# Packing masked score triangles of sliding-window attention as 64-key halves on 32x64 array tiles

## The chip, the cores and the metric

The kernel runs on one core of one Trainium2 chip. The metric is the device time of one launch in microseconds. Times quoted are medians of several runs. A ratio is the mean time of one kernel's runs over that of the other's of the same rounds, so it is not quite the ratio of the medians quoted beside it. Intervals are 95% intervals.

## The reference

A transformer layer on 2048 tokens of width 1024: layer norm, attention with 32 heads of 32 columns in which a query sees itself and the 255 keys before it, output projection, residual; then layer norm, a feed-forward block of width 3584 with silu, residual. Everything is bf16.

```python
scores = jnp.einsum("bhqd,bhkd->bhqk", q, k) * (Dh ** -0.5)
idx = jnp.arange(S)
mask = (idx[:, None] - idx[None, :] >= 0) & (idx[:, None] - idx[None, :] < W)   # W = 256
p = _softmax(jnp.where(mask[None, None], scores, -1e9), axis=-1)
o = jnp.einsum("bhqk,bhkd->bhqd", p, v)
# ...
h = x + _A_ref(_layernorm(x, axis=-1), A_wqkv, A_wo)
h2 = h + _B_ref(_layernorm(h, axis=-1), B_w1, B_w2)
```

## The kernel before

The tokens are four blocks of 512, numbered 0 to 3. The attention of block b is spread over the dense matmuls of another stage: those that make Q, K and V of block b + 1, and, for block 3, the output projection of blocks 0 to 2. Each such stage has 24 dense groups of 8 matmuls with 512 columns. Between the groups stand **score bursts** (keys times queries for four heads at once, on four 32-row tiles of the array), the exp on ScalarE, the masking selects on GpSimd, and the **output matmuls** (128x33, probabilities times values).

For 128 queries there are three chunks of 128 keys. The middle one is not masked; the first and the last are, each on one side of its diagonal. A group of four heads has 12 chunks of scores, which fill three bursts of 512 columns, called A, B and C:

```python
PIECES = {
    "A": [(0, 0, 3, 0), (-2, 0, 1, 3)],       # key tile, first query tile, tiles, column
    "B": [(-1, 0, 2, 0), (2, 2, 2, 2)],
    "C": [(3, 3, 1, 0), (1, 1, 3, 1)],
}
def scores(b, g, kind):
    for kt, q0, nq, ch in PIECES[kind]:
        t = b * 4 + kt
        for hh in range(4):
            r0 = hh * DH
            nc.tensor.matmul(sc[hh // 2][:, hh % 2, ch * P:(ch + nq) * P],
                             lhsT=kT[t // 4][r0:r0 + DH, g, (t % 4) * P:(t % 4 + 1) * P],
                             rhs=qT[b][r0:r0 + DH, g, q0 * P:(q0 + nq) * P],
                             start=True, stop=True, tile_position=(r0, 0))
    for pair in range(2):                      # two heads of 512 columns each
        nc.scalar.activation(out=e, in_=sc[pair], func=ACT.Exp, scale=scale)
        # ... selects for the masked chunks
```

The stage of block 3: its dense groups are the output projection. Each pair of groups makes one 128-row tile of h, which VectorE adds to the residual and the DMA queue of SyncE (SP) stores to DRAM. Four tiles of h are read back as one transfer of 1 MB for the layer norm of the first feed-forward block.

```python
def wo_group(b, j, c):                         # residual tile b*4+j, column half c
    # ... 8 dense matmuls into one of two accumulators
    nc.vector.tensor_tensor(out=t_out[j % 2][...], in0=acc, in1=r_in[(b * 4 + j) % 6][...], op=ALU.add)
    if c == 1:
        late.append(lambda: nc.sync.dma_start(out=h_dram[...], in_=t_out[j % 2]))
# ... stage of block 3, n counts its 24 groups
run_late()                                     # queued stores and transposes, first of all
if n % 2 == 0 and n >= 2 and n // 2 + 5 < S // P: load_res(n // 2 + 5) # a residual tile
scores(NB - 1, g, kind)
wo_group(*dense[n])
if pending: pending.pop(0)()                   # a piece of output matmuls
if n in (1, 4, 7, 12, 15): load_w1(...)        # 896 KB of weights each
if n == 9: steps = ln2_steps(0); steps.pop(0)()   # the 1 MB read of h
for _ in range(1 if n < 16 else 2):            # layer norm steps of the first feed-forward block
    if steps and n >= 12: steps.pop(0)()
```

The softmax here doesn't subtract the row's maximum and nothing guards it: scores larger than these inputs give would overflow.

Of the kernel before, what the change touches and what calls it, by code (L numbers as in the profile page):

```python
# [14 lines left out]
P = 128  # L15
# [3 lines left out]



PIECES = {
    "A": [(0, 0, 3, 0), (-2, 0, 1, 3)],
    "B": [(-1, 0, 2, 0), (2, 2, 2, 2)],
    "C": [(3, 3, 1, 0), (1, 1, 3, 1)],
}
CHUNKS = [
    [(-2, "A", 3), (-1, "B", 0), (0, "A", 0)],
    [(-1, "B", 1), (0, "A", 1), (1, "C", 1)],
    [(0, "A", 2), (1, "C", 2), (2, "B", 2)],  # L30
    [(1, "C", 3), (2, "B", 3), (3, "C", 0)],
]
KINDS = "ABC"


def first_stream(n_groups):
# [12 lines left out]
def kernel(  # L49
# [37 lines left out]
    r_t = big.tile([P, 4096], BF16, name="r_t")  # L87
    r_o = big.tile([P, 8192], BF16, name="r_o")
    r_a = big.tile([P, 49664], BF16, name="r_a")
    r_e = big.tile([P, 12288], BF16, name="r_e")  # L90
    r_n = big.tile([P, 1536], BF16, name="r_n")

    ps_tp = tc.tile_pool(name="ps_tp", bufs=1, space=bass.MemoryType.PSUM, reuse_waits="tile")
# [5 lines left out]
    def view(region, off, *dims):  # L99
        n = 1  # L100
        for d in dims:
            n *= d
        ap = region[:, off:off + n]
        if len(dims) == 2:
            return ap.rearrange("p (a b) -> p a b", b=dims[1])
        if len(dims) == 3:
            return ap.rearrange("p (a b c) -> p a b c", b=dims[1], c=dims[2])
        return ap
# [15 lines left out]
    w2_off = 18432  # L124
    w2 = [view(r_a, w2_off + 4096 * s, 4, D) for s in W2_SLOT]
    ebuf = [view(r_e, 1024 * i, 2, 512) for i in range(12)]
    obuf = [view(r_n, 512 * i, 4, P) for i in range(3)]
    h_blk = [view(r_a, w2_off + 4096 * 4, 4, D)] + [view(r_e, 8192, 4, D)] * 3
    ln2T = [view(r_a, w2_off + 4096 * 5, KT, 512), view(r_e, 0, KT, 512), view(r_e, 4096, KT, 512), view(r_e, 0, KT, 512)]
# [103 lines left out]
    def v_group(b, j, c, copy, between=None):  # L233
        acc = next_acc()
        for kt in range(KT):
            if between:
                between(kt)
            nc.tensor.matmul(acc, lhsT=lnT_b[b % 2][:, kt, j * P:(j + 1) * P], rhs=wv[:, kt, c * 512:(c + 1) * 512],  # L238
                             start=(kt == 0), stop=(kt == KT - 1))
        copy(out=v[:, b * 4 + j, c * 16:(c + 1) * 16, 0:DH], in_=acc.rearrange("p (h d) -> p h d", d=DH))  # L240

    def qk_group(b, which, g, copy, between=None):
        acc = next_acc()
        col0 = which * D + g * P
        for kt in range(KT):
            if between:
                between(kt)
            nc.tensor.matmul(acc, lhsT=wqk[:, kt, col0:col0 + P], rhs=lnT_b[b % 2][:, kt, :],  # L248
                             start=(kt == 0), stop=(kt == KT - 1))
        copy(out=(qT, kT)[which][b][:, g, :], in_=acc)  # L250
# [10 lines left out]
        while late:  # L261
            late.pop(0)()

    def wo_group(b, j, c):
        acc = next_acc()
        for g in range(G):
            nc.tensor.matmul(acc, lhsT=qT[b][:, g, j * P:(j + 1) * P], rhs=wo[:, g, c * 512:(c + 1) * 512],  # L267
                             start=(g == 0), stop=(g == G - 1))
        nc.vector.tensor_tensor(out=t_out[j % 2][:, c * 512:(c + 1) * 512], in0=acc,
                                in1=r_in[(b * 4 + j) % 6][:, c * 512:(c + 1) * 512], op=ALU.add)  # L270
        if c == 1:
            late.append(lambda: nc.sync.dma_start(out=h_dram[(b * 4 + j) * P:(b * 4 + j + 1) * P, :], in_=t_out[j % 2]))


    def e_of(i, kind, pair):
        return ebuf[(i * 6 + KINDS.index(kind) * 2 + pair) % 12]

    first_bursts, first_where = first_stream(G)

    def scores(b, g, kind):  # L280
        for kt, q0, nq, ch in PIECES[kind]:
            t = b * 4 + kt
            for hh in range(4):
                r0 = hh * DH
                nc.tensor.matmul(  # L285
                    sc[hh // 2][:, hh % 2, ch * P:(ch + nq) * P],
                    lhsT=kT[t // 4][r0:r0 + DH, g, (t % 4) * P:(t % 4 + 1) * P],
                    rhs=qT[b][r0:r0 + DH, g, q0 * P:(q0 + nq) * P],
                    start=True, stop=True, tile_position=(r0, 0),
                )  # L290
        for pair in range(2):
            e = e_of(b * G + g, kind, pair)
            nc.scalar.activation(out=e, in_=sc[pair], func=ACT.Exp, scale=scale)  # L293
            if kind == "A":
                mask(e, 0, 1, True)
                mask(e, 2, 2, False)
            elif kind == "B":
                mask(e, 1, 1, False)
                mask(e, 2, 1, True)
            else:  # L300
                mask(e, 0, 2, True)
                mask(e, 3, 1, False)

    def scores_first(n):
        ch = 0
# [19 lines left out]
                    mask(e, ch, 1, kt == q)  # L325

    def mask(e, c0, n, upper):
        ap = e[:, :, c0 * P:(c0 + n) * P].rearrange("p h (c q) -> p h c q", q=P)
        sgn = 1 if upper else -1
        nc.gpsimd.affine_select(out=ap, in_=ap, pattern=[[0, 2], [0, n], [sgn, P]],  # L330
                                compare_op=ALU.is_ge if upper else ALU.is_gt,
                                fill=0.0, base=0, channel_multiplier=-sgn)

    def attn_out(b, g, first, last):
        i = b * G + g
        for n in range(first, last):
            pair, qt, hh = n // 8, n // 2 % 4, n % 2
            for m, (kt, kind, ch) in enumerate(CHUNKS[qt]):
                nc.tensor.matmul(  # L339
                    o_ps[pair][:, qt * 2 + hh, 0:VW],  # L340
                    lhsT=e_of(i, kind, pair)[:, hh, ch * P:(ch + 1) * P],
                    rhs=v[:, b * 4 + kt, g * 4 + pair * 2 + hh, :],
                    start=(m == 0), stop=(m == 2),
                )
            if n % 8 == 7:
                attn_norm(i, pair)
# [26 lines left out]
    def attn_transpose(b, g):  # L373
        i = b * G + g
        nc.sync.dma_start_transpose(out=qT[b][:, g, :].rearrange("p (t q) -> p t q", q=P),
                                    in_=obuf[i % 3].rearrange("p t d -> p (t d)"))

    def tail_of(b, g):
        def end():
            attn_out(b, g, 11, 16)  # L380
            late.append(lambda: attn_transpose(b, g))
        return [lambda: attn_out(b, g, 0, 5), lambda: attn_out(b, g, 5, 11), end]

    dve, act = nc.vector.tensor_copy, nc.scalar.copy

# [71 lines left out]
    for j in range(4):  # L457
        load_x(2, j)
    steps, turns = ln1_steps(2)
    pending = []  # L460
    count = [0, 0]

    def between(kt):
# [21 lines left out]


    for b in range(2, NB):
        dense = [lambda j=j, c=c: v_group(b, j, c, dve) for j in range(4) for c in range(2)]
        dense += [lambda w=w, g=g: qk_group(b, w, g, dve) for g in range(G) for w in range(2)]
        if b + 1 < NB:  # L490
            for j in range(4):
                load_x(b + 1, j)
            steps, turns = ln1_steps(b + 1)
        else:
            steps, turns = [], []
            nc.sync.dma_start(out=wo[:, 0:4, :], in_=wo_v[:, 0:4, :])
            nc.sync.dma_start(out=wo[:, 4:8, :], in_=wo_v[:, 4:8, :])
            load_res(0)
            load_res(1)
        n = 0  # L500
        for g in range(G):
            for kind in KINDS:
                run_late()
                if b == NB - 1 and n in (4, 10, 14):
                    load_w1({4: 7, 10: 6, 14: 5}[n])
                scores(b - 1, g, kind)
                dense[n]()
                if pending:
                    pending.pop(0)()
                if steps and n >= 1 and n != 3:  # L510
                    steps.pop(0)()
                elif turns and n % 3 == 2:
                    turns.pop(0)()
                n += 1
            pending = tail_of(b - 1, g)
        assert not steps and not turns


# [5 lines left out]
    for t in range(2, 6):  # L524
        load_res(t)
    steps = []
    n = 0
    for g in range(G):
        for kind in KINDS:
            run_late()  # L530
            if n % 2 == 0 and n >= 2 and n // 2 + 5 < S // P:
                load_res(n // 2 + 5)
            scores(NB - 1, g, kind)
            wo_group(*dense[n])
            if pending:
                pending.pop(0)()
            if n in (1, 4, 7, 12, 15):
                load_w1((1, 4, 7, 12, 15).index(n))
            if n == 9:
                steps = ln2_steps(0)  # L540
                steps.pop(0)()
            if n == 17:
                nc.sync.dma_start(out=w2[0], in_=w2_v[:, 0:4, :])
            for _ in range(1 if n < 16 else 2):
                if steps and n >= 12:
                    steps.pop(0)()
            n += 1
        pending = tail_of(NB - 1, g)
    while steps:
        steps.pop(0)()  # L550

# [101 lines left out]
```

## Time and profile before

| | before |
|---|---|
| time, median of 3 | 696.89 us (696.79 to 697.0) |
| span of the profiled run | 695.5 us |
| TensorE clock granted | 1.000 |
| bursts in blocks 1 to 3 | 72, 8 matmuls each |
| last residual group to first feed-forward matmul | no wait |

Lines of the page, the timeline and the waits of this kernel are shown in the prediction. In a timeline line the columns are start and length in us, engine, source line, operation, what it writes and reads, shapes, the number of instructions merged, and in brackets the idle time before and what ended it.

### The profile page before, as it was taken

The numbers are of one execution on the slowest core, as the hardware profiler recorded it, in microseconds if no ns is written. First come the engines' busy times: TensorE is split into PE (matmuls) and PEld (weight loads), VectorE is DVE, ScalarE is ACT, GpSimd is POOL, SyncE is SP. The second block draws the span as 40 slices with busy tenths as digits, with TensorE's granted clock in tenths as the row PEclk, the third lists the DMA queues.
The fourth block names the chain that finished last, engine by engine and source line by source line (L and its number), as shares of the span: only waits on it lengthen the run. The fifth ranks groups of instructions, "written<-read, shape, count | busy, mean of one in ns | idle before, by whom it ended". The sixth has DMA issues, their size and how long they took to land.

```text
span 695.5 us, 12334 instructions
## 1 busy us (share of the span) xinstructions
PE 690.1 (99%) x5091; PEld 331.6 (48%) x5091; DVE 289.5 (42%) x616; ACT 257.9 (37%) x328; POOL 174.5 (25%) x391
## 2 busy tenths in 40 slices
PE   8999999999999999999999999999999999999998
PEld 3444444555555555544444444444444444444445
DVE  6267646644443448544316134433133251244111
ACT  4326657777777777621310023300033100233000
POOL 1007667777777777500000000000000000000000
PEclk9999999999999999999999999999999999999999
DMA  7732131026231778880123410024200023100110
GB/s 241 257 53 77 35 93 51 17 60 193 70 124 23 205 251 272 199 311 31 31 76 99 107 38 1 1 83 77 83 1 1 11 95 91 45 1 1 30 39 24
DMA packets 76457, 60.84 MB, mean 87 GB/s; under 512 B 50288, under 2 KB 60528, under 8 KB 76400
## 3 DMA queue, kind: packets, MB, share of 16 engines
q1 hardware_dynamic: 76256, 59.78, 29.9%
q8 instruction: 40, 0.66, 0.4%
q10 hardware_dynamic: 144, 0.26, 0.1%
q14 instruction: 17, 0.14, 0.1%
HBM read 39.85 MB, written 8.39 MB: 69 GB/s over the span
## 4 chain that ended last, share of the span: by engine, by line
PE 99%; DMA 1%; DVE 0%; issue 0%
PE hacc L563 19%; PE hacc L600 17%; PE acc L248 16%; PE acc L600 10%; PE acc L563 9%; PE acc L238 8%; PE acc L267 7%; PE o_ps L339 4%; PE sc L285 3%; PE hacc L267 1%; PE o_ps L354 1%; PE sc L313 1%; DMA r_o<-in_A_x_dram 1%; PE tp L216 0%; DVE ln_st L169 0%; DVE r_o L197 0%
## 5 line engine op out<-in xcount | busy, mean ns | idle before, releaser
L330 POOL TENSOR_SCALAR_AFFINE_SELECT r_e<-r_e 128x256 bf16<-128x256 bf16 (+1 forms) x384 | 171.6, 477 | 116.5 <-ACT r_e L322 65.1
L293 ACT ACTIVATE r_e<-sc 128x1024 bf16<-128x1024 f32 x144 | 139.5, 1021 | 45.1 <-PE sc L285 31.0
L600 PEld LDWEIGHTS <-r_a 128*128 128x128 bf16 x952 | 90.9, 98 | 103.0
L563 PEld LDWEIGHTS <-r_w 128*128 128x128 bf16 x896 | 87.4, 98 | 104.8
L600 PE MATMUL hacc<-r_a 128*128 128x512 bf16 (+2 forms) x616 | 122.5, 360 | 0.0
L563 PE MATMUL hacc<-r_e,r_w 128*128 128x512 bf16 x456 | 100.9, 379 | 0.0
L572 ACT ACTIVATE r_n<-hacc 128x512 f32<-128x512 f32 x30 | 17.9, 597 | 178.9 <-PE hacc L563 178.9
L600 PE MATMUL acc<-r_a 128*128 128x512 bf16 x336 | 74.0, 379 | 0.0
L248 PEld LDWEIGHTS <-r_w 128*128 128x128 bf16 x512 | 46.5, 97 | 57.1 <-issue 7.0
L250 DVE CAST r_a<-acc 128x512 bf16<-128x512 f32 x56 | 38.7, 691 | 72.9 <-PE acc L248 56.3
L248 PE MATMUL acc<-r_t,r_w 128*128 128x512 bf16 x256 | 60.0, 379 | 0.0
L248 PE MATMUL acc<-r_w 128*128 128x512 bf16 x256 | 58.2, 380 | 0.0
L267 PE MATMUL acc<-r_o,r_a 128*128 128x512 bf16 x208 | 49.4, 380 | 0.0
L563 PE MATMUL acc<-r_e,r_w 128*128 128x512 bf16 x216 | 49.1, 379 | 0.0
L339 PEld LDWEIGHTS <-r_e 128*128 128x128 bf16 x1152 | 39.5, 96 | 17.0
L322 ACT ACTIVATE r_e<-sc 128x1024 bf16<-128x1024 f32 x36 | 34.9, 1021 | 21.2 <-PE sc L313 20.1
L339 PE MATMUL o_ps<-r_a,r_e 128*128 128x33 bf16 x1152 | 40.2, 178 | 0.0
L615 DVE SCALAR_TENSOR_TENSOR r_t<-hacc,r_t 128x512 bf16<-128x512 f32 (+2 forms) x22 | 14.0, 635 | 56.7 <-PE hacc L600 56.7
L267 PEld LDWEIGHTS <-r_a 128*128 128x128 bf16 x256 | 23.1, 98 | 29.6 <-issue 5.1
L615 DVE SCALAR_TENSOR_TENSOR r_t<-acc,r_t 128x512 bf16<-128x512 f32 x12 | 8.3, 692 | 64.2 <-PE acc L600 64.2
L573 DVE SCALAR_TENSOR_TENSOR r_a<-r_n,hacc 128x512 bf16<-128x512 f32 x30 | 20.6, 688 | 33.0 <-ACT r_n L572 33.0
L563 PE MATMUL hacc<-r_a,r_w 128*128 128x512 bf16 x144 | 32.9, 379 | 0.0
(71 smaller groups left out, 476.5 us busy)
## 6 DMA issues: line engine op xcount, KB each, us to landing
r_w<-in_B_w_dram SPq DMA_DIRECT2D x8, 896.0 KB, 5.1
r_a<-in_B_w_dram SPq DMA_DIRECT2D x7, 1024.0 KB, 7.9
r_w<-in_A_wqkv_dram SPq DMA_DIRECT2D x6, 1024.0 KB, 8.7
h_dram<-r_t SPq DMA_DIRECT2D x16, 256.0 KB, 3.0
r_t<-h_dram SPq DMA_DIRECT2D x16, 256.0 KB, 2.8
out_dram<-r_t SPq DMA_DIRECT2D x31, 128.0 KB, 1.7
r_o<-in_A_x_dram SPq DMA_DIRECT2D x15, 256.0 KB, 4.0
r_e<-h_dram SPq DMA_DIRECT2D x3, 1024.0 KB, 5.7
```

The costliest lines, as they stand in the source:

```text
L238: nc.tensor.matmul(acc, lhsT=lnT_b[b % 2][:, kt, j * P:(j + 1) * P], rhs=wv[:, kt, c * 512:(c + 1) * 512], start=(kt == 0), stop=(kt == KT ...
L248: nc.tensor.matmul(acc, lhsT=wqk[:, kt, col0:col0 + P], rhs=lnT_b[b % 2][:, kt, :], start=(kt == 0), stop=(kt == KT - 1))
L250: copy(out=(qT, kT)[which][b][:, g, :], in_=acc)
L267: nc.tensor.matmul(acc, lhsT=qT[b][:, g, j * P:(j + 1) * P], rhs=wo[:, g, c * 512:(c + 1) * 512], start=(g == 0), stop=(g == G - 1))
L285: nc.tensor.matmul(sc[hh // 2][:, hh % 2, ch * P:(ch + nq) * P], lhsT=kT[t // 4][r0:r0 + DH, g, (t % 4) * P:(t % 4 + 1) * P], rhs=qT[b][r0 ...
L293: nc.scalar.activation(out=e, in_=sc[pair], func=ACT.Exp, scale=scale)
L322: nc.scalar.activation(out=e, in_=sc[pair], func=ACT.Exp, scale=scale)
L330: nc.gpsimd.affine_select(out=ap, in_=ap, pattern=[[0, 2], [0, n], [sgn, P]], compare_op=ALU.is_ge if upper else ALU.is_gt, fill=0.0, base ...
L339: nc.tensor.matmul(o_ps[pair][:, qt * 2 + hh, 0:VW], lhsT=e_of(i, kind, pair)[:, hh, ch * P:(ch + 1) * P], rhs=v[:, b * 4 + kt, g * 4 + pa ...
L563: nc.tensor.matmul(acc, lhsT=w1[:, kt, ft * P:(ft + 1) * P], rhs=ln2T[b][:, kt, :], start=(kt == 0), stop=(kt == KT - 1))
L600: nc.tensor.matmul(acc[:, 0:c1 - c0], lhsT=gT[:, ft, j * P:(j + 1) * P], rhs=w2[ft // 4][:, ft % 4, c0:c1], start=(ft == 0), stop=(ft == F ...
L615: nc.vector.scalar_tensor_tensor(out=t_out[j % 2][:, c0:c1], in0=acc[:, 0:c1 - c0], scalar=0.5, in1=t_in[j % 2][:, c0:c1], op0=ALU.mult, o ...
```

## The change

A masked 128x128 triangle has one dead 64x64 square: on the diagonal it is the later 64 keys with the earlier 64 queries, at the far edge of the window the earlier 64 keys with the later 64 queries. The change computes each half of the keys on its own 32x64 array tile, without the dead square, so that a pair of triangles, one of each kind, needs 192 columns of a bank in place of 256. Two kinds of burst come of it: X and Y (odd) with four triangles and one unmasked chunk, and C with unmasked chunks of two head groups. A block needs 20 bursts, not 24. Each X or Y burst has 24 matmuls and two exps per pair of heads. The bursts are also hung evenly inside the dense groups, by a counter, instead of between them, and so are the output matmuls.

```diff
+    def scores_xy(b, g, odd):
+        parts = [
+            (mid, 0, q0, q0 + 320, 64), (mid, 1, q0 + 64, q0 + 384, 128),
+            (last, 0, q0 + 256, q0 + 384, 384), (first, 1, q0, q0 + 128, 0),
+            (first, 0, q0, q0 + 64, 0), (last, 1, q0 + 320, q0 + 384, 448),
+        ]
+        for step in range(3):
+            for hh in range(4):
+                for kt, half, qa, qb, col in parts[step * 2:step * 2 + 2]:
+                    ...
+                    nc.tensor.matmul(
+                        sc[hh // 2][half * 64:half * 64 + 64, hh % 2, col:col + qb - qa],
+                        lhsT=kT[t // 4][r0:r0 + DH, g, k0:k0 + 64],
+                        rhs=qT[b][r0:r0 + DH, g, qa:qb],
+                        start=True, stop=True, tile_position=(r0, half * 64),
+                    )
+        for pair in range(2):
+            nc.scalar.activation(out=tri[:, :, :, 64:256], in_=both, func=ACT.Exp, scale=scale)
+            nc.scalar.activation(out=..., in_=bank[:, :, 192:320], func=ACT.Exp, scale=scale)
+            select(four[:, :, 0:P], four[:, :, 64:64 + P], False)
+            select(four[:, :, P:2 * P], four[:, :, P:2 * P], True)
...
+        def between(self, kt):                  # before every dense matmul
+            if self.seen * 20 >= self.done * 192:
+                run_late()
+                self.bursts[self.done]()
+                self.done += 1
+            if self.seen * 40 >= (self.given * 2 + 1) * 192:
+                ...                             # one piece of output matmuls
+            self.seen += 1
...
-            run_late()
             if n % 2 == 0 and n >= 2 and n // 2 + 5 < S // P:
                 load_res(n // 2 + 5)
-            scores(NB - 1, g, kind)
-            wo_group(*dense[n])
-            if pending:
-                pending.pop(0)()
+        wo_group(*dense[n], stream.between)
```

## The prediction

> **What bounds the kernel now.** I read the page's engine totals first, then the chain that ended last.
>
> ```profile
> PE 690.1 (99%) x5091; PEld 331.6 (48%) x5091; DVE 289.5 (42%) x616; ACT 257.9 (37%) x328; POOL 174.5 (25%) x391
> PE 99%; DMA 1%; DVE 0%; issue 0%
> ```
>
> TensorE is busy for 99% of the span and is 99% of the chain. The granted clock is 1.000. So the time is the sum of what TensorE spends, and the change is worth what it takes out of that sum, unless it creates a wait. Busy time doesn't show the spacing of pipelined matmuls, so I read the timeline of one attention step in block 2 next (columns: start, length, engine, line, operation, operands, count).
>
> ```profile
> 203.16 0.61 PE L339 MATMUL o_ps<-r_a,r_e 128*128 128x33 bf16 x18
> 203.70 0.40 PE L285 MATMUL sc<-r_a 32*128 32x128 bf16 x8
> 204.03 1.41 PEld L248 LDWEIGHTS <-r_w 128*128 128x128 bf16 x8 [0.21 <-issue]
> 204.03 1.90 PE L248 MATMUL acc<-r_t,r_w 128*128 128x512 bf16 x8
> 204.22 1.94 ACT L293 ACTIVATE r_e<-sc 128x1024 bf16<-128x1024 f32 x2 [0.67 <-PE sc L285]
> 205.31 1.98 POOL L330 TENSOR_SCALAR_AFFINE_SELECT r_e<-r_e 128x512 bf16<-128x512 bf16 x4 [0.90 <-ACT r_e L293]
> 205.77 0.54 PE L339 MATMUL o_ps<-r_a,r_e 128*128 128x33 bf16 x15
> 206.24 0.40 PE L285 MATMUL sc<-r_a 32*128 32x384 bf16 x8
> 206.57 1.68 PE L248 MATMUL acc<-r_t,r_w 128*128 128x512 bf16 x7
> ```
>
> The step repeats: eight dense matmuls, 15 or 18 output matmuls, one score burst. The dense weight load after a burst had to stand for 0.21 us: nothing of the next shape begins under the burst's tail. From the start times of the single matmul records I take a tariff, start to start:
> - dense 512-column matmul: 216 ns; output matmul: 25.4 ns; dense to output and output to dense add nothing.
> - into a burst: 109.5 ns after the last output matmul, so 84 ns beyond its own 25. Where the first stream (line 313) enters from a dense matmul it is 312 ns, 96 beyond its 216.
> - first burst matmul to next foreign matmul: 330 ns with 8 matmuls (two waves of four row tiles), 333 with 12 (three waves). 512 columns would stream in 213 ns.
> - the first dense matmul after a burst is followed after 225 ns, 9 too many.
>
> So one burst costs 84 + 330 + 9 = 423 ns, of which only 213 is streaming. 72 bursts in blocks 1 to 3 are 30.5 us, 4.4% of the time. That is all the change can act on.
>
> Last I read who waits, since a burst can only start when ScalarE has emptied both score tiles:
>
> ```profile
> ACT r_e L293 <- PE sc L285: 31.0, 49, 0.7
> ACT r_e L293 <- POOL r_e L330: 14.1, 23, 1.1
> PEld L285 <- issue: 1.1, 3, 0.4
> ```
>
> ScalarE waits for TensorE, hardly the other way. But the margin is thin: a burst's first exp starts 513 ns after it, the two exps start 920 ns apart, the second lasts 1021, so ScalarE ends at 2454; most bursts follow at 2530. In one place, at the start of block 1, a burst came 2163 ns after the last and its third matmul was held for 337 ns; it started 52 ns after ScalarE's end. Needed: 2506; margin 24 ns.
>
> **What the Trainium skill says.** "TensorEngine Tiling (Array Packing)", Key Properties, says that changing the tiling mode drains TensorE while tiles within a mode run independently. The trace agrees: 84 to 96 ns lost going in, about 100 going out. The same page, Tile-to-Partition Mapping, Restrictions, says that column tiling switches off Fast Weight Load; no load of the kernel before is column tiled (all carry 128 columns), so this trace can't say what it costs. "TensorE: Matmul & The Clock Gate", Part 3, gives a pack's span as one matmul plus about 4 ns per further tile, for row and column tiles alike; this trace has 3 to 4 ns between the starts of row tiles. "PSUM — Partial Sum Buffer", PSUM bank collisions, allows different column tiles to write one bank at once in different partitions, which the new packing relies on; nothing here shows it yet.
>
> **The change, part by part.**
>
> *Fewer bursts.* A block has 20 instead of 24: 4 of unmasked chunks (C) and 16 of triangles (X and Y). A masked triangle's lower and upper 64 keys each have a dead 64-query half; giving each half its own 32x64 tile puts two triangles in 192 columns. The output matmuls (384 a block) and dense matmuls (192 a block) stay.
>
> *A C burst* has 16 matmuls, four waves of 128 columns. From 330 and 333 for two and three waves: 336. It is now entered from a dense matmul, because bursts are hung inside the dense groups after 9 or 10 matmuls. 96 + 336 + 9 = 441 ns.
>
> *An X or Y burst* has 24 matmuls in three waves on eight tiles: 320, 128 and 64 columns, again 512 = 213 ns. In the 384|128 burst the last matmul starts at 183 = 160 + 13 at the wave change + 10 stagger; in a three-wave burst the changes and stagger together add 26 ns too (186 = 53 + 107 + 26). With eight tiles the stagger is 7 x 3.7 = 26 instead of 10, so the last start is 133 + 53 + 16 + 26 = 228. After a last start come its 27 ns and the 94 ns of exit (330 - 183 - 53): 349. The weight loads lose the fast path. By the first page named (P/1.2) 64 columns take 53 ns; I let 16 of this show, as the second wave's loads lie under the first wave's 133 ns, and put the burst at 365. That 16 is a choice, the weakest number here. 96 + 365 + 9 = 470 ns.
>
> *Sum.* 12 x 441 + 48 x 470 = 5.3 + 22.6 = 27.9 us against 30.5: 2.6 us off the path. A block loses four bursts (1.7 us), but gives back about half in dearer bursts. The 0.34 us hold at the start of block 1 should go, as no two bursts have fewer than nine dense matmuls between them. 2.9 in all: 694.0. I add 0.2 for some wait I don't see: 694.2.
>
> *ScalarE.* The exp of 1024 columns takes 1021 ns, tanh of 512 takes 597, so 0.828 ns a column and 173 fixed; back to back 101 of that overlap. An X burst has four exps, 768 and 256 columns per pair: 708 + 284 + 708 + 385 = 2085 ns from first start to end, against 1941 now. Starting at about 545, it ends at 2630; with 52, the next burst may start at 2680. The shortest spacing is nine dense matmuls with 15 output matmuls: 365 + 9 + 9 x 216 + 381 + 96 = 2795. It fits, with 115 to spare. Total ScalarE falls: 49 to about 43 us a block.
>
> *GpSimd.* Two selects of 512 elements on each pair, 590 ns apart each: 2.4 us an X burst, none on C, in a spacing of about 3.0. In the three blocks 288 selects become 192 (24 bursts of 4 a block; 16 of 4), all of the long form. Output pieces run three bursts behind their first data, over 1 us after the selects are done. The exp ring is two groups deep, and the last reader of a slot precedes its next writer. Both lie beside TensorE.
>
> **The rivals.**
> 1. *Weight loads bind.* 24 loads without the fast path, two per row strip, may serialise: 6 x 27 ns in a strip, or 53 each. The third wave's loads wait for the second, which lasts only 53 ns. Against: skill's span model, and eight row-tile loads today start 4 ns apart. If so, X bursts cost some 445 ns or more and the gain is eaten: 698.
> 2. *ScalarE becomes the bound.* Splitting each exp adds 72 ns twice a burst; if strided PSUM reads are slower or GpSimd delays a write, the 115 ns vanish at the shortest-spaced bursts, one in five. At 0.2 us each for 12 to 15 of them, up to 3 us: time 697. For: the present margin is only 24 ns. Against: the spacing grows with the burst.
> 3. *The drain is smaller in the new mode, or loads hide wholly.* X bursts near 333: 48 x 32 ns less, 692.6.
> 4. *VectorE late with a copy*, since bursts no longer separate dense groups evenly. The first stream already runs so and shows no TensorE wait on VectorE: little.
>
> **Range and chances.** Rivals 1 and 3 give 698 and 692.5; I give 2 and 4 about one in five together, at up to 3 us. Predicted 694.2, 8 in 10 between 691.8 and 697.8. Two per cent is 13.9 us: to gain it, almost half of all burst time would have to vanish; to lose it, each X burst would have to cost 340 ns more. Faster 0.01, same 0.97, slower 0.02.
>
> **What would show it right or wrong.** In the profile after: 1344 matmuls at the score lines in place of 576; X bursts from first to next foreign matmul near 365 (349 to 400 right, over 430 is rival 1, with gaps between waves); C near 336; entry 96; 60 bursts; no matmul of a burst held in mid wave for ScalarE (that is rival 2); dense spacing still 216; exps of 768 at about 809 ns and 256 at about 385. The prediction is wrong if the column tiles don't run at once, doubling 213 ns of streaming: 48 x 0.2 = 10 us more, 704.

## More of the kernel before

One more place is needed for comparison later, the end of block 3's stage on TensorE's timeline (line 267 is the output projection, 563 the first feed-forward matmul):

```profile
288.42 1.90 PE L267 MATMUL acc<-r_o,r_a 128*128 128x512 bf16 x8
290.16 0.53 PE L339 MATMUL o_ps<-r_a,r_e 128*128 128x33 bf16 x15
290.54 1.89 PE L563 MATMUL acc<-r_a,r_w 128*128 128x512 bf16 x8
```

The three follow one another without a bracket: nothing is waited for. By the trace's records the last transpose of the first feed-forward layer norm landed 1.05 us before the matmul that reads it.

## The result

697.1 us median (696.73 to 697.58, 4 runs) against 696.85 (696.79 to 697.0, 4 runs). The ratio is 1.0004, interval 0.9986 to 1.0021. The clock was 1.000 in all four runs. The time lies inside the range. But 694.2 was expected and about 2.9 us did not arrive.

The page of the profile after, engine totals and the chain that ended last:

```profile
PE 687.7 (99%) x5859; PEld 330.0 (47%) x5859; DVE 292.0 (42%) x616; ACT 240.7 (35%) x400; POOL 161.6 (23%) x295
PE 94%; DVE 2%; DMA 1%; issue 1%; POOL 1%; SPq 0%; ACT 0%; DVEq 0%; POOLq 0%
```

TensorE is 94% of the chain where it was 99%: VectorE, a DMA and GpSimd are now on it. The timeline of a step in block 3 shows the new burst working as meant (line 302 is an X or Y burst, 314 and 315 its exps, 368 the selects):

```profile
244.88 0.43 PE L302 MATMUL sc<-r_a 32*64 32x320 bf16 x24
...
245.25 1.25 PE L271 MATMUL acc<-r_o,r_a 128*128 128x512 bf16 x5
...
245.48 0.81 ACT L314 ACTIVATE r_e<-sc 128x768 bf16<-128x768 f32 x1 [1.13 <-PE sc L302]
...
246.19 0.38 ACT L315 ACTIVATE r_e<-sc 128x256 bf16<-128x256 f32 x1
...
246.36 2.63 POOL L368 TENSOR_SCALAR_AFFINE_SELECT r_e<-r_e 128x512 bf16<-128x512 bf16 x4 [3.35 <-ACT r_e L314]
```

From burst to next dense matmul 0.37 us pass (244.88 to 245.25): column tiles do run at once. Now the stages, from start times of single matmul records in the two profiled runs:

| stretch, us | before | after | difference |
|---|---|---|---|
| start of the span to first burst | 50.82 | 50.63 | -0.19 |
| first burst to first group of the output projection | 178.76 | 176.55 | -2.22 |
| output projection (block 3) to first feed-forward matmul | 60.96 | 63.64 | +2.68 |
| from there to the last matmul | 401.88 | 401.88 | 0.00 |

Blocks 1 and 2 gained 2.2 us. Block 3 lost them again. In it four gaps between matmuls are too long for any of the tariff's entries; less the usual 216 ns they are 0.55, 0.30, 0.75 and 2.13 us, 3.7 together. Without them block 3 would have gained about 1.05 us, as the other two did. Two of the four on TensorE's timeline:

```profile
262.63 1.02 PE L271 MATMUL acc<-r_o,r_a 128*128 128x512 bf16 x4 [0.39 <-DVE r_t L273]
...
290.81 1.89 PE L614 MATMUL acc<-r_a,r_w 128*128 128x512 bf16 x8 [1.97 <-issue]
```

The first waits for a residual add on VectorE (line 273) to free an accumulator. The second is the first feed-forward matmul. The bracket says "issue", that is, the profile saw no releaser; but the last layer norm transpose it reads landed 0.20 us before it. Behind the first stands this, in the chain in order of time, and on VectorE's timeline:

```profile
255.14 6.66 DMA h_dram<-r_t
261.79 0.03 issue
261.82 0.02 DVEq L273
```

```profile
261.89 0.69 DVE L273 TENSOR_TENSOR r_t<-acc,r_a 128x512 bf16<-128x512 f32 x1 [4.11 <-PE o_ps L377]
```

VectorE stood idle for 4.11 us. The bracket names the output matmuls, which had long been done; the chain names the right one: the store of h tile 4 was issued at 255.14 and landed at 261.79, and the add needs the output tile that it was reading. After that VectorE works through adds and layer norm statistics in order with hardly a pause until 275 us, and TensorE waits for it once more, 0.30 us at 275.35. The third hold, 0.75 us at 283.57, is not this backlog but another store:

```profile
282.82 0.69 DVE L273 TENSOR_TENSOR r_t<-acc,r_a 128x512 bf16<-128x512 f32 x1 [1.98 <-PE sc L302]
```

VectorE was idle again. The store of tile 8 was issued at 277.00, 1.70 us after its add, and landed at 282.75; the add of tile 10, which needs the same output tile, started 0.08 us later. The layer norm's last normalising operation (line 199) stands behind this add on VectorE, so that the late stores delay the feed-forward matmul too. Why was tile 4's store issued so late? The queue of SP, before and then after (line 256/258 loads a residual tile, 272/276 stores h, 433/497 is the 1 MB read of h):

```profile
250.11 0.33 SPq L272 DMA_DIRECT2D h_dram<-r_t  x1
250.48 0.43 SPq L256 DMA_DIRECT2D r_t<-in_A_x_dram  x1
253.33 1.20 SPq L375 DMA_TRANSPOSE r_a<-r_n  x1
254.71 0.45 SPq L433 DMA_DIRECT2D r_a<-h_dram  x1
255.26 0.44 SPq L272 DMA_DIRECT2D h_dram<-r_t  x1
```

```profile
248.04 0.33 SPq L258 DMA_DIRECT2D r_t<-in_A_x_dram  x1
248.42 0.43 SPq L276 DMA_DIRECT2D h_dram<-r_t  x1
250.72 1.20 SPq L413 DMA_TRANSPOSE r_a<-r_n  x1
254.16 0.38 SPq L497 DMA_DIRECT2D r_a<-h_dram  x1
254.63 0.46 SPq L258 DMA_DIRECT2D r_a<-in_A_x_dram  x1
255.14 0.42 SPq L276 DMA_DIRECT2D h_dram<-r_t  x1
```

Before, a store went out 0.03 us after its add, in 11 cases of 12. After, it stands behind the residual load, and behind whatever else the queue waits on: 0.40 to 3.80 us after its add. Tile 4's store at 255.14 was 2.48 us late, behind a read that waits for tile 3 to land.

### The profile page after: what moved, and what is told of

The parts are those of the page before. It is cut to its first block, busy times and chain, and to the rows that moved or that the text cites. A ratio compares the mean times of both kernels' runs of the same rounds, so it can differ in the third digit from the quotient of the medians.

```text
span 695.9 us, 13820 instructions
## 1 busy us (share of the span) xinstructions
PE 687.7 (99%) x5859; PEld 330.0 (47%) x5859; DVE 292.0 (42%) x616; ACT 240.7 (35%) x400; POOL 161.6 (23%) x295
## 4 chain that ended last, share of the span: by engine, by line
PE 94%; DVE 2%; DMA 1%; issue 1%; POOL 1%; SPq 0%; ACT 0%; DVEq 0%; POOLq 0%
PE hacc L614 19%; PE hacc L651 17%; PE acc L250 16%; PE acc L651 10%; PE acc L614 9%; PE acc L240 8%; PE acc L271 4%; PE o_ps L377 3%; PE sc L302 2%; PE hacc L271 1%; PE o_ps L392 1%; DVE ln_st L171 1%; DMA h_dram<-r_t 1%; PE sc L348 1%; DVE r_t L273 1%
## 5 line engine op out<-in xcount | busy, mean ns | idle before, releaser
L368 POOL TENSOR_SCALAR_AFFINE_SELECT r_e<-r_e 128x512 bf16<-128x512 bf16 (+1 forms) x288 | 158.6, 568 | 127.6 <-ACT r_e L357 64.9
L614 PEld LDWEIGHTS <-r_w 128*128 128x128 bf16 x896 | 87.4, 98 | 107.2 <-issue 2.4
L314 ACT ACTIVATE r_e<-sc 128x768 bf16<-128x768 f32 x96 | 78.2, 814 | 49.9 <-PE sc L302 49.9
L250 PEld LDWEIGHTS <-r_w 128*128 128x128 bf16 x512 | 44.9, 97 | 47.3 <-issue 0.2
L250 PE MATMUL acc<-r_t,r_w 128*128 128x512 bf16 x256 | 61.7, 379 | 0.0
L250 PE MATMUL acc<-r_w 128*128 128x512 bf16 x256 | 59.9, 379 | 0.0
L271 PE MATMUL acc<-r_o,r_a 128*128 128x512 bf16 x208 | 52.4, 379 | 1.1 <-DVE r_t L273 1.0
L377 PEld LDWEIGHTS <-r_e 128*128 128x128 bf16 x1152 | 37.8, 96 | 14.2
L357 ACT ACTIVATE r_e<-sc 128x1024 bf16<-128x1024 f32 x36 | 34.9, 1021 | 21.2 <-PE sc L348 20.1
L377 PE MATMUL o_ps<-r_a,r_e 128*128 128x33 bf16 x1152 | 38.3, 178 | 0.0
L315 ACT ACTIVATE r_e<-sc 128x256 bf16<-128x256 f32 x96 | 37.6, 392 | 0.0
```

Source lines behind the costliest of these rows:

```text
L250: nc.tensor.matmul(acc, lhsT=wqk[:, kt, col0:col0 + P], rhs=lnT_b[b % 2][:, kt, :], start=(kt == 0), stop=(kt == KT - 1))
L271: nc.tensor.matmul(acc, lhsT=qT[b][:, g, j * P:(j + 1) * P], rhs=wo[:, g, c * 512:(c + 1) * 512], start=(g == 0), stop=(g == G - 1))
L314: nc.scalar.activation(out=tri[:, :, :, 64:256], in_=both, func=ACT.Exp, scale=scale)
L315: nc.scalar.activation(out=e[:, 1024:1280].rearrange("p (h q) -> p h q", q=P), in_=bank[:, :, 192:320], func=ACT.Exp, scale=scale)
L368: nc.gpsimd.affine_select(out=dst, in_=src, pattern=[[0, n] for n in dst.shape[1:-1]] + [[sgn, P]], compare_op=ALU.is_ge if upper else ALU ...
L377: nc.tensor.matmul(o_ps[pair][:, qt * 2 + hh, 0:VW], lhsT=chunk_of(i, bank, piece, pair, hh), rhs=v[:, b * 4 + kt, g * 4 + pair * 2 + hh, ...
```

## The experiments

Two theories at first. **A**: the flush moved behind other transfers, stores are late, they hold adds, adds hold TensorE. **B**: the stage is bound by the DMA engines or by the layer norm chain whatever the order; TensorE just arrives 2.4 us earlier and waits longer. All twelve runs gave a result; each was run in the same rounds as the kernel before. "Changed" below means the kernel after the change. "FF wait" is the wait before the first feed-forward matmul in the profiled run, from its matmul records: the gap less 0.22 us, or less 0.025 where an output matmul stands before it (e4, e8).

| run | median (range), us | ratio to before (interval) | TensorE held by adds | FF wait, us |
|---|---|---|---|---|
| changed | 697.1 (696.73 to 697.58) | 1.0004 (0.9986 to 1.0021) | 1.6 us | 2.13 |
| e1 flush on top | 696.16 (694.88 to 697.84) | 0.9997 (0.9984 to 1.001) | no | 1.24 |
| e2 store at once | 698.1 (696.26 to 698.23) | 1.0017 (1.0005 to 1.003) | no | 2.70 |
| e3 third tile | 694.5 (693.96 to 695.84) | 0.9971 (0.9958 to 0.9985) | no | 1.18 |
| e4 before, flush inside | 696.68 (696.25 to 696.89) | 1.0000 (0.9988 to 1.0013) | no | 0 |
| e5 flush on top, norm ahead | 694.76 (694.31 to 695.24) | 0.9971 (0.9959 to 0.9984) | no | 0.89 |
| e6 changed, light W1 | 695.58 (694.67 to 698.09) | 0.9989 (0.9973 to 1.0004) | no | 1.60 |
| e7 all three remedies | 693.89 (693.43 to 694.56) | 0.9957 (0.9945 to 0.9969) | no | 0.29 |
| e8 before, light W1 | 696.6 (696.46 to 696.96) | 0.9997 (0.9985 to 1.0009) | no | 0.24 |
| e9 e2 again | 697.9 (696.76 to 698.39) | 1.0006 (0.9991 to 1.002) | no | 2.83 |
| e10 e2, wait filled | 697.33 (696.26 to 698.12) | 1.0001 (0.999 to 1.0013) | no | 0, filled |
| e11 changed, norm ahead | 696.44 (695.58 to 699.52) | 0.9999 (0.9981 to 1.0017) | 1.6 us | 0.59 |
| e12 third tile, norm ahead | 694.72 (693.76 to 695.32) | 0.9964 (0.9951 to 0.9977) | no | 0 |

The kernel before took 696.59 (e1 to e4), 696.79 (e5 to e8), 696.94 (e9, e10) and 696.9 us (e11, e12) in these rounds. Some of these traces lack a few of the matmul records; the waits are read where the records stand.

**e1: flush on top.** From the changed kernel, in the loop of block 3:

```diff
     for n in range(24):
+        run_late()
         if n % 2 == 0 and n >= 2 and n // 2 + 5 < S // P:
```

> The changed kernel with one line more: in block 3 the queued stores and transposes are flushed at the head of each group, ahead of the residual load, as in the kernel before. Theory A (the change moved the h stores behind other transfers in the one DMA queue; late stores hold VectorE's residual adds, these hold the accumulators and TensorE): stores are issued within 0.1 us of their add again instead of 0.4 to 3.8, adds start about 0.42 us after their last matmul, the 3.7 us of TensorE holds in block 3 fall under 0.7 us, time 693.6 to 694.4. Theory B (block 3 is bound by what the 16 DMA engines can move, or by the layer norm chain of the first feed-forward block; arriving earlier only means waiting longer): adds or the first feed-forward matmul still wait some 3 us, time 696.3 to 697.2.

Five of the twelve stores went out 0.03 us after their add again, the others 0.46 to 1.38 and one 3.80; no matmul of the projection was held by an add any more. That is A's half. But the first feed-forward matmul still waited 1.24 us, B's half, and the time, 694.88 in the profiled run, was up to 697.84 in others. Neither theory had said that the spread would grow to 3 us.

**e2: store at once.** From the changed kernel:

```diff
         if c == 1:
-            late.append(lambda: nc.sync.dma_start(out=h_dram[...], in_=t_out[j % 2]))
+            nc.sync.dma_start(out=h_dram[...], in_=t_out[j % 2])
```

> The changed kernel with each h store issued right after its second add, ahead of the weight loads and of the 1 MB read of h that the queue holds at that place, further forward than in the kernel before. Theory A: as the run with the flush on top or a little better, since the store of tile 4 no longer stands behind the read of h that waits for tile 3: 693.3 to 694.2, no hold of TensorE over 0.3 us in block 3. Theory B: 696.3 to 697.2, the holds move to the first feed-forward matmul.

A miss for A. The adds were free, and the time was worse than before: the wait had moved whole to the feed-forward matmul, 2.70 us, as B had it. The trace says where this layer norm was late, its last normalising operation first and then the queue of SP (line 203 is a layer norm transpose, 413 one of the attention):

```profile
280.04 0.54 DVE L199 TENSOR_SCALAR r_a<-r_a,st_b,rs_b 128x1024 bf16<-128x1024 bf16 x1
```

```profile
280.63 1.87 SPq L203 DMA_TRANSPOSE r_a<-r_a  x1
282.61 1.22 SPq L413 DMA_TRANSPOSE r_a<-r_n  x1
283.93 1.12 SPq L276 DMA_DIRECT2D h_dram<-r_t  x1
285.10 2.65 SPq L203 DMA_TRANSPOSE r_a<-r_a  x2
```

VectorE was done at 280.58, but the last two transposes were issued from 285.10 on, behind three others that follow one another with pauses of 0.1 us at most. Here the one queue, and not VectorE, held the end of the chain. This is a reading of the trace; no run moved that order alone.

**e3: third output tile.** From the changed kernel, the sixth residual tile becomes a third output tile:

```diff
+    t_third = view(r_a, 23552, 1024)
+    def t_wo(t):
+        return t_out[t % 2] if t >= 12 else [*t_out, t_third][t % 3]
+    def r_slot(t):
+        return 1 if t == 14 else t % 5
-        nc.vector.tensor_tensor(out=t_out[j % 2][...], in0=acc, in1=r_in[(b * 4 + j) % 6][...], op=ALU.add)
+        nc.vector.tensor_tensor(out=t_wo(b * 4 + j)[...], in0=acc, in1=r_in[r_slot(b * 4 + j)][...], op=ALU.add)
# ... the residual loads one tile less ahead
```

> The changed kernel with a third output tile for the residual adds of block 3 (and one residual tile fewer), so that an add waits for the store of three tiles before, not two; the order in the DMA queue stays. Theory A: the stores remain 0.4 to 3.8 us late but nobody waits for them; adds lag 0.42 us; what may stay is part of the 2.1 us wait of the first feed-forward matmul. Time 693.8 to 695.3. Theory B: TensorE waits the same 3 us, at the first feed-forward matmul: 696.3 to 697.2.

As A said. The stores stay late and no one waits for them: 694.5. TensorE's timeline of this run, at the feed-forward matmul, names what is left:

```profile
288.33 1.89 PE L622 MATMUL acc<-r_a,r_w 128*128 128x512 bf16 x8 [1.02 <-DMA r_a<-r_a]
```

The DMA `r_a<-r_a` is the layer norm's last transpose.

**e4: the kernel before with the flush inside the group**, at the places of the changed kernel:

```diff
-            run_late()
             ...
-            wo_group(*dense[n])
+            wo_group(*dense[n], mid_late)     # run_late() every 9 or 10 dense matmuls
```

> The kernel before, old bursts, with only the flush of stores and transposes in block 3 moved into the group, behind the residual load, at the places where the changed kernel has it. Theory A: stores issued 0.4 us and more after their add instead of 0.03; some adds late; TensorE is slower here and so hides part: 0.3 to 2.5 us slower than before, 697.2 to 699.4. Theory B: order doesn't matter, 696.8 to 697.1.

A missed: 696.68 against 696.59. Eleven of the stores were 0.40 to 2.92 us late, 0.72 in the mean of all twelve against 1.48 after the change, so the edit made only half of the lateness. Even so the first adds of tiles 6 and 10 were held by a store (they started 0.08 us after it landed, that of tile 6 about 1 us late), and it cost nothing. So late stores alone aren't the cause. With the old bursts TensorE needs the accumulators up to 2.4 us later. But little was left: the last transpose landed 0.20 us before the feed-forward matmul, not 1.05.

This gave **theory C**: block 3's stage holds a second path beside TensorE, h stores, read of h, statistics, normalising, transposes, that ended 1.05 us before it was needed. Making TensorE 3.3 us faster runs into it, first at the adds, then at the feed-forward matmul.

**e5: layer norm steps ahead**, on top of e1:

```diff
-        for _ in range(1 if n < 16 else 2):
+        for _ in range(1 if n < 16 else 2 if n < 18 else 3):
             if steps and n >= 12:
```

> The run with the flush on top, and the last steps of the first feed-forward block's layer norm given three to a group from group 18 on, so that its last two transposes are queued one group (2.5 us) earlier. Theory C, formed from the first four runs: the residual adds are one victim of late stores, but once they are free the first feed-forward matmul waits for the last transpose of that layer norm, whose chain (h stores, 1 MB read of h, statistics, normalising, transposes) runs through the busy DMA engines and so differs from run to run by some 3 us; that is why runs of the flush on top spread from 694.9 to 697.8 where the kernel before spreads by 0.5. If so the wait before that matmul (1.2 us in the profiled run) shrinks to under 0.3 us and the median falls to 693.5 to 695.5 with a smaller spread. Theory D, that something else slows the unprofiled runs: median stays near 696.2.

The median fell by 1.4 us and the spread from 3.0 to 0.9, as C says. The wait shrank to 0.89 us only, where C had it under 0.3. C's reason for the spread, transfers that differ from run to run, is not what was found later (e9).

**e6 and e8: light W1**, on the changed kernel and on the kernel before. Results are wrong on purpose (relative error 0.042 in both):

```diff
     def load_w1(kt):
-        nc.sync.dma_start(out=w1[:, kt, :], in_=w1_v[:, kt, :])
+        cols = F if kt > 4 else F // 8
+        nc.sync.dma_start(out=w1[:, kt, 0:cols], in_=w1_v[:, kt, 0:cols])
```

> The changed kernel itself, order untouched, with the five W1 slices that are read in block 3 cut to an eighth of their columns (wrong results on purpose): 3.9 MB less traffic beside the h stores. If the DMA engines' load is what makes late stores costly, the adds wait no longer and the last transpose lands before TensorE asks: holds under 0.7 us, time 693.3 to 694.3, spread under 0.5 us. If the order in the queue alone is the cause, whatever the load, the stores still go out 0.4 us and more late and some 2 to 3 us of holds stay: 695.5 to 697.

> The kernel before with the same cut W1 reads (wrong results on purpose), as the control of the light run: TensorE bounds it and no wait on a DMA reaches it, so all theories say 696.3 to 696.9, as before. If it gained over 0.5 us, the kernel before was held by these transfers too and the light run would prove less.

With seven eighths of these loads gone no add held TensorE, although the order was the changed one. The adds were not quite free: those of tiles 6 and 10 still started 0.08 to 0.09 us after a store landed, that of tile 6 about 0.6 us late. In part the stores went out earlier: tile 3's landed after 3.24 us, not 5.67, so the read of h that waits for it, and tile 4's store behind that read, were issued sooner, 1.44 us after the add and not 2.48. So this traffic is part of why a store is late. The wait before the feed-forward matmul stayed, 1.60 us, so it isn't the W1 traffic that sets it. The last transposes are issued with group 21, behind an attention transpose, and the last takes 2.9 us to land even here. The time, 695.58 with a spread of 3.4 us, lies in the second range of the expectation but not for its reason: no add held anything. The control behaved: the kernel before gains 0.2 us, inside its interval. (Its feed-forward matmul was held too, by 0.24 us, starting 0.20 us after the last transpose landed: there is little slack in that join.)

**e7: all three remedies**: e3, e1's flush and e5's steps together.

> The version with all three remedies: third output tile, flush on top, layer norm steps ahead. Theory C: 693.3 to 694.3 with a spread under 1 us, the 3.2 us that the bursts save, less what is left of the wait before the first feed-forward matmul. Theory D: no better than the third tile alone, 694 to 695.

C's number: 693.89, ratio 0.9957 (0.9945 to 0.9969), 3.0 us faster than before. Its results are right. The chain that ended last on its page is TensorE's alone again:

```profile
PE 99%; DMA 0%; DVE 0%; issue 0%
```

**e9 and e10: why the spread?** The runs of e1, e2 and e6 above 697 us all have a mean granted clock of 0.997 or 0.998; the others 0.999 or 1.000. **Theory E**: the wait costs twice, as TensorE's clock drops after it. e9 is e2 unedited; e10 adds:

```diff
     run_late()
     load_w2(5)
+    for i in range(12):
+        nc.tensor.matmul(acc_banks[2 + i % 4], lhsT=wo[:, 0, 0:P], rhs=wo[:, 0, 0:512], start=True, stop=True)
```

> The store-at-once kernel once more, unedited, to catch a slow run with its trace: of its five runs the one profiled at a full clock took 696.26, the four others 697.96 to 698.23 with a mean granted clock of 0.997 to 0.998. Theory E: when TensorE stands idle long enough before the first feed-forward matmul, its clock is granted at a half for some us after it, so a wait of 2.7 us costs near 2 us more. Then most runs are again near 698.1 with a clock of 0.997 to 0.998, and a trace of one shows the half clock beginning at that wait, with dense matmuls 427 ns apart for a few us. If the clock loss lies elsewhere (the start, the end), theory E is wrong and the slow runs have longer waits only.

> The store-at-once kernel with 12 dense matmuls into unused accumulators, their results never read, before the first feed-forward matmul: 2.6 us of work in the place of the 2.7 us wait. Theory E: the clock stays at 1.000 in all runs, the first feed-forward matmul is not later, and the time falls to 695.5 to 696.6 with a spread under 1 us, although TensorE does more. If the slow runs came from longer DMA waits alone, the fill changes nothing or costs up to 2.6 us: 698 to 700.

The profiled run of e9 was a slow one (698.39). The table of stretches for it (from:to in us, TensorE busy and instructions, granted clock, DMA share, GB/s) and TensorE's timeline:

```profile
285.00:290.00 5.00, 2.43 (x33) 1.00 0.97 253
290.00:295.00 5.00, 4.90 (x29) 0.66 0.74 246
295.00:300.00 5.00, 5.00 (x54) 1.00 0.01 3
```

```profile
290.10 2.94 PE L614 MATMUL acc<-r_a,r_w 128*128 128x512 bf16 x8 [2.67 <-issue]
```

After 2.67 us of idling the clock is 0.66 over the next 5 us; eight dense matmuls take 2.94 us where they took 1.89. The clock records say 0.5 for 3.413 us, from 0.7 us after the start of that matmul. From it to the last matmul this run took 403.41 us, all others 401.88: 1.5 us more. In the profiled run of e2 the wait was about as long and the clock stayed at 1.0:

```profile
289.63 1.89 PE L614 MATMUL acc<-r_a,r_w 128*128 128x512 bf16 x8 [2.54 <-issue]
```

E10's clock was 1.000 in all six runs, against 0.997 or 0.998 in seven of the nine runs of e2 and e9, so filling the wait keeps it up. The fill takes the wait's place (line 629):

```profile
287.21 2.75 PE L629 MATMUL hacc<-r_o 128*128 128x512 bf16 x12
289.80 1.89 PE L614 MATMUL acc<-r_a,r_w 128*128 128x512 bf16 x8
```

The time, 697.33, is only 0.6 us under e9's, not the 1.5 and more expected, and spreads by 1.9: on this chip the kernel before itself ran from 696.44 to 698.96 at full clock. Within e9 the run at full clock took 696.76, the three others 697.56 to 698.39. E's mechanism is shown, its size against the kernel before isn't. The changed kernel itself isn't touched by it: its four runs have a clock of 1.000, as its waits are shorter and spread over four places.

**e11 and e12: which remedies are needed.** e11 is the changed kernel with e5's edit alone, e12 is e3 with e5's edit.

> The changed kernel with only the layer norm steps given three to a group from group 18 on; queue order and two output tiles as changed. If the late stores at the residual adds come first and the late layer norm is in part their consequence (VectorE does both in order), the adds still lag by some 2 us, 1.6 us of holds stay in block 3 and VectorE has no room to be earlier: 696.0 to 697.2. If the layer norm chain alone were the cause: 693.8 to 695.0.

> The changed kernel with the third output tile and the layer norm steps ahead, but the order in the DMA queue as changed (no flush on top). If the order matters only through the adds' wait on stores, this equals the version with all three remedies: 693.6 to 694.4, wait before the first feed-forward matmul under 0.6 us. If the flush order also delays the layer norm's read of h, 0.5 to 1 us more: 694.5 to 695.2.

In e11 the adds hold TensorE exactly as in the changed kernel (0.57, 0.31 and 0.75 us at the same places), and the time stays. In e12 no wait is left, with the flush still inside the group; the wait before the feed-forward matmul is nil:

```profile
286.19 1.02 PE L278 MATMUL acc<-r_o,r_a 128*128 128x512 bf16 x4
287.05 1.89 PE L622 MATMUL acc<-r_a,r_w 128*128 128x512 bf16 x8
```

Its ratio, 0.9964 (0.9951 to 0.9977), can't be told from that of e7, 0.9957 (0.9945 to 0.9969); the two ran on different chips. Its median, 694.72, lies in the second range of the expectation, the one for a read of h delayed by the order. The traces don't show that delay: the read was issued 25.06 us after the stage began and landed at 31.6, in e7 at 24.93 and 32.3. So the third tile and the earlier layer norm are enough to clear every wait; the order of the queue need not be changed, once no one waits for the stores. That both are needed is read from the waits alone (1.18 us left in e3, 0.89 in e5): the ratios of e3 and e5, both 0.9971, can't be told from that of e12.

## Why the prediction was right or wrong

The midpoint was 2.9 us too low. That the range still held it is luck: its upper part was made for rivals 1 and 2 (698 and 697), and the loss came from neither.

**The bursts: right.** An X or Y burst takes 359 ns to the next dense matmul (365 said), entered in 93 (96 said); a C burst 335 (336 said). Twenty burst spacings take 60.29 us in the steady part; before, 24 took 61.37. That is 1.09 us a block, 3.3 in three (2.6 said). The split of the X burst can't be checked as it was written: the second wave starts at 160 ns, not 146, and the last matmul at 239, not 228. The burst is thus 10 ns above the 349 worked out without slower weight loads; whether these or the change of waves take them, no run shows. (Nor does a trace show the 53 ns of rival 1.) The streaming rate that the prediction takes, 213 ns for 512 columns, fits the trace of the kernel before: waves of 128, 256 and 384 columns were followed by the next after 66, 119 and 174 ns, 54 ns more for each 128. The prediction's "lower and upper 64 keys each have a dead 64-query half" is loose, as a triangle has one dead square; its 192 columns for two triangles are right.

**Rivals 1 and 3: ruled out** at their sizes (445 ns and more, near 333) by the same 359 ns.

**ScalarE (rival 2): mostly right.** Exps of 768 columns took 814 ns (809 said), of 256 took 392 (385 said). They start 595 ns after the burst instead of 545, so the margin at the shortest spacing is 77 ns, not 115; no burst in the steady part was held. "49 to about 43 us a block" mixes exps counted with and without their overlap: with it the terms give 46.6 and 41.1. The pages show 5.7 us a block less.

**"The 0.34 us hold at the start of block 1 should go": wrong.** 0.29 us of it stayed. The reason given, nine dense matmuls between bursts, left out that no output matmuls stand there yet. That spacing is 2405 ns, below the 2680 worked out two lines further on.

**"I add 0.2 for some wait I don't see" is the step that failed**, and with it the short word on rival 4, "VectorE late with a copy: little". It measured 3.7 us: 1.6 at residual adds, 2.1 at the first feed-forward matmul. VectorE was late not with a copy but with the residual adds, since stores held its output tiles; and the layer norm of the first feed-forward block was late. "Unless it creates a wait" was the prediction's own condition, and it was looked at for ScalarE, GpSimd and VectorE's copies, not for the stores. Two things were overlooked: that the flush of stores moved behind the residual load, which stands in the diff, and that with TensorE at 99% other paths can still have only 1 us of slack. Late stores did no harm alone (e4, at half the lateness). Removing the add waits without also bringing the layer norm forward left a wait at its end (e1, e2, e3). With both dealt with the predicted saving appears: 3.0 us in e7 against 2.9, which is the 3.3 of the bursts less the 0.29 us that e7 still waits.

**What stays open.** What decides whether a run of e2 loses its clock after a wait of about 2.7 us wasn't tested. The clock records of the two traces suggest where the wait falls: in every trace that has them, the changes of the clock lie whole multiples of 3.413 us apart. Drawn out over the kernel, one such stretch of e9 runs from 287.37 to 290.78 and held 2.7 us of the wait; in e2 the wait was split, 1.2 us in one stretch and 1.5 in the next. That is two traces, not a rule. How much of the wait before the feed-forward matmul is the order of the transposes in SP's queue (e2) is open too. Where the rest of e6's spread comes from wasn't traced either: two of its six runs had the lower clock, the others still differ by 1 us.

## What to carry to other kernels

A kernel bound by one engine at 99% may have a second path ending a microsecond earlier; before counting a gain on the first, follow the second to its join and read its slack there. Moving code into another loop also moves the transfers that it issues, and one late store holds its buffer, the adder behind it and the engine behind that. If a join is left that TensorE reaches too early, the wait can also cost the clock.

## What the Trainium skill lacked or had wrong

- "TensorEngine Tiling (Array Packing)", Key Properties, says that a mode change drains TensorE, without a size. Here: 84 to 96 ns into a burst (93 for 32x64 tiles), about 94 ns beyond streaming out of it, and about 10 ns on the second dense matmul.
- The same page, Tile-to-Partition Mapping, Restrictions, says that column tiling disables Fast Weight Load. That page gives no size. Here 64-column loads take 101 to 105 ns in the records against 90 to 95 for 128 columns on row tiles; most of this is overlapped, and the burst of 24 such loads took 359 ns, 10 more than the prediction's working gives without slower loads. What part of the 10 is theirs wasn't tested.
- "TensorE: Matmul & The Clock Gate", Part 3, gives a span for one pack of tiles, about 4 ns a further tile. Eight tiles start 3.3 ns apart, in agreement. It says nothing on packs in sequence: 320-column tiles (133 ns) were followed by the next wave after 160 ns.
- The same page, Part 1, has the clock fall to a half after one or more idle windows of about 3.4 us. Here idling of 2.67 us before one matmul was enough in the profiled run, and the half clock lasted 3.413 us. With 2.54 us in another run the clock stayed up; "What stays open" has where the two waits fell.
